# Dilated attention scores as 64-row matmuls instead of zero-padded 128-row ones, with two output banks in an expert layer

## The chip, the cores and the metric

The kernel runs on one core of a Trainium2 chip. The metric is the device time of one execution in microseconds (us). The kernel before takes 339.29 us, the median of three runs (339.09 to 340.91). The profile comes from one execution each time, so it has a span of its own (337.9 us for the kernel before, from the first to the last instruction).

A word used throughout: a **visit** is a stretch of consecutive matmuls that read only 64 (or fewer) of the 128 partitions, with matmuls over more than 64 partitions before and after it.

## The reference, cut to what matters

Eight batches of eight heads, 576 positions, head dimension 64. Heads 0 to 3 attend to the last 32 positions (here called plain), heads 4 to 7 to every fourth of the last 128 (dilated). The result goes through an expert layer with a swish of its own beta for each unit.

```python
def _attn_ref(q, k, v):                       # each 8 x 8 x 576 x 64, values x 0.1
    scores = np.matmul(q, k.transpose(0, 1, 3, 2)) / np.sqrt(64)
    rel = pos[:, None] - pos[None, :]
    mask_plain = (rel >= 0) & (rel < 32)
    mask_dil = (rel >= 0) & (rel < 128) & (rel % 4 == 0)
    ...                                       # masked softmax over keys
    return np.matmul(attn, v)

def _moe_ref(x, w_in, w_out, beta):           # x: 4608 x 512, w_in: 512 x 2048
    h = x @ w_in
    g = h * (1.0 / (1.0 + np.exp(-beta * h)))
    return g @ w_out
```

## The kernel before

The program is a fixed order of small steps. An attention batch is a list of step names: K and Q bring keys and queries (batches 0 and 1 by transposes on TensorE), `S` makes scores, `V` multiplies by values, `X` transposes the result into `xT`; `k`, `q`, `d`, `v` are copies on other engines, and W is a warm-up matmul whose result nobody reads. Batch 0 runs alone in the prologue; the batches after it are woven between the matmuls of the expert layer, whose nine stages of 512 tokens each begin with `h_ps` blocks (TensorE), a tanh (ScalarE) and a product g (VectorE), and end with `o_ps` blocks. The numbers in a step name are the pair of heads (2 and 3 are the dilated pairs) and the part of it.

```python
STEPS = (
    "S20 S21 S22 k0 S23 k1 V20 S30 q0 V21 S31 q1 V22 S32 q2 V23 S33 q3 V30 X20 S00 V31 S01 X21 V32 "
    "S02 V33 S10 V00 X30 S11 V01 S12 X31 V10 X00 V11 X01 X10 X11"
).split()
...
    psum_h = psum("psum_h", 2)
    psum_o = psum("psum_o", 1)      # one bank for output blocks
    psum_at = psum("psum_at", 5)    # five rotating banks for all of attention
```

Two dilated heads lie on the two halves of the partitions, 64 rows each. A score matmul uses all 128 rows: its keys are both heads' rows, and its queries are in `qzd`, where the other head's half is zero. One matmul of 192 columns then yields both heads. The price is the zeros, and the copies that spread the queries:

```python
    def spread_dil(b, hf, eng):
        rows = slice(64 * hf, 64 * hf + 64)
        copy_on(eng)(out=qzd[b % 2][rows, hf], in_=raw[b, "d"][rows])

    def step_q(b, x):
        tv = [transposes_p("q", y) for y in (x, x + 1)] if x < 2 else transposes_d("q", x)
        h = slice(2 * (x - 2), 2 * (x - 2) + 2)
        for n, hf in ((0, 0), (1, 1), (0, 1), (1, 0)):
            rows = slice(64 * hf, 64 * hf + 64)
            out = (q1[b][rows, x + n, hf].rearrange("p (a e) -> p a e", e=9) if x < 2 else
                   qzd[b][rows, hf, n, h].rearrange("p h (a w) -> p h a w", w=3))
            copy_on(nc.scalar if hf else nc.vector)(out=out, in_=tv[n][rows])

    def step_s(b, x, j):
        sc = bank().rearrange("p (a n) -> p a n", a=2)
        if x < 2:
            n, K, c = QT, P, 4 * QT * j
            mask = mask_p["PP" if j else "FP"][:].rearrange("p a b e u -> p a (b e u)")
        else:
            hf, rp = divmod(j, 2)
            n, K, c = DQ[hf], DK[hf], 4 * (hf * 2 * DQ[0] + rp * DQ[hf])
            mask = mask_d[hf][:].rearrange("p a b n -> p a (b n)")
        if b < 2:
            rhs = neg_d[hf][0:K].unsqueeze(1).to_broadcast([K, 4, n]) if x > 1 else (
                neg_p[:, 1:2].to_broadcast([K, 4, n]) if j else
                neg_p[:].unsqueeze(2).to_broadcast([K, 2, 2, n]))
            nc.tensor.matmul(sc[0:K, :, 0:2 * n], lhsT=ident_b[0:K, 0:K], rhs=rhs,
                             start=True, stop=False)
        for a in range(2):
            if x < 2:
                i = 2 * j + a
                if b < 2:
                    nc.tensor.matmul(
                        sc[:, a, 0:2 * n], lhsT=k1[b][:, x, i * QT:i * QT + P],
                        rhs=q1[b][:, x, :, i * QT:(i + 1) * QT], start=False, stop=a == 1)
                    continue
                for h2 in range(2):
                    h4 = 2 * x + h2
                    nc.tensor.matmul(
                        sc[:, a, h2 * n:(h2 + 1) * n],
                        lhsT=kz[b % 2][:, h4, i].rearrange("p e u -> p (e u)"),
                        rhs=qq[b % 2][:, h4, i].rearrange("p e u -> p (e u)"),
                        start=True, stop=True)
            else:
                h4 = 2 * (x - 2) + a
                nc.tensor.matmul(
                    sc[0:K, a, 0:2 * n],
                    lhsT=kd[b][:, rp, h4, DO[hf]:DO[hf] + K],
                    rhs=qzd[b % 2][:, :, rp, h4, hf * DQ[0]:hf * DQ[0] + n],
                    start=b > 1, stop=b > 1 or a == 1)
        w = pt[x][0:K, c:c + 4 * n].rearrange("p (a n) -> p a n", a=2)
        nc.scalar.activation(out=w, in_=sc[0:K, :, 0:2 * n], func=ACT.Exp, scale=SCALE)
        if b > 1:
            nc.gpsimd.tensor_tensor(out=w, in0=w, in1=mask[0:K], op=ALU.mult)
```

The two matmul groups of the expert layer, with the output block that goes into the single `o_ps` bank and is evicted by ScalarE:

```python
    def slot_h(t, fb, kts=None):
        if (t, fb) not in h_t:
            h_t[t, fb] = (bank() if (t == 0 or t == 1 and fb < 7) and fb % 3 else
                          psum_h.tile([P, NTOK], FP32, name="h_ps")[:])
        hps = h_t[t, fb]
        for kt in kts or (2, 3, 0, 1):
            nc.tensor.matmul(
                hps, lhsT=w_in_bf[:, kt, fb * P:(fb + 1) * P],
                rhs=xT[:, kt, t * NTOK:(t + 1) * NTOK],
                start=(kt == 2), stop=(kt == 1))
        if kts == (2, 3):
            return
        tnh = tnh_pool.tile([P, NTOK], BF16, name="tnh")
        nc.scalar.activation(
            out=tnh[:], in_=hps, func=ACT.Tanh, scale=beta_half[:, fb:fb + 1])
        g = g_pool.tile([P, NTOK], BF16, name="g")
        nc.vector.scalar_tensor_tensor(
            out=g[:], in0=tnh[:], scalar=1.0, in1=hps, op0=ALU.add, op1=ALU.mult)
        g_t[t, fb] = g

    ...

    def slot_o(t, tb, part):
        if part == 0:
            if t == NTT - 1 and tb % 2 or t == 0 and tb < 2:
                o_t[t, tb] = psum_h.tile([P, HD], FP32, name="h_ps")
            else:
                o_t[t, tb] = psum_o.tile([P, HD], FP32, name="o_ps")
        ops = o_t[t, tb]
        for fb in range(4 * part, 4 * part + 4):
            nc.tensor.matmul(
                ops[:], lhsT=g_t[t, fb][:, tb * P:(tb + 1) * P], rhs=w_out_bf[:, fb, :],
                start=(fb == 0), stop=(fb == NFB - 1))
        if part == 3:
            osb = osb_pool.tile([P, HD], FP32, name="osb")
            nc.scalar.mul(out=osb[:], in_=ops[:], mul=0.5)
            later.append([2, lambda: store(t * NTOK + tb * P, osb)])
```

The softmax here doesn't subtract the row's maximum and nothing guards it: scores larger than these inputs give would overflow.

## Time and profile before

| | kernel before |
|---|---|
| time, median of 3 | 339.29 us |
| span of the profiled run | 337.9 us |
| TensorE (PE) busy | 317.3 us, 94% |
| VectorE (DVE), ScalarE (ACT), GpSimd (POOL) busy | 58%, 59%, 39% |
| a settled batch (from about 132 us on) | 33.6 us |

The main views are shown in the prediction below, and each is explained there. Two further readings are needed for the result. The first is the clock row of the page: the span in 40 equal slices of some 8.4 us, each digit the granted TensorE clock in tenths of full speed.

```profile
PEclk9969999999999999999999999999999999999999
```

The 6 says that the third slice ran partly at half clock; the trace's clock records give 16.6 to 23.4 us. The second is the timeline of ScalarE at the first tanh, which ends the prologue: everything that delays it delays the whole kernel.

```profile
28.18 0.69 ACT L504 ACTIVATE tnh<-h_ps,beta_half 128x512 bf16<-128x512 f32 x1 [0.47 <-PE h_ps L497]
```

The columns of a timeline row are the start in us, the time to its end in us, engine, source line, operation, output and inputs, shapes, the number of instructions in the row, and in brackets how long the engine was idle before it and what ended that. The first tanh of each stage is a good milestone: its time in two traces, subtracted, shows in which stage time was lost.

### The profile page before, as it was taken

How to read it: one execution, taken by the hardware profiler on the slowest of the kernel's cores; microseconds unless marked ns; L12 is line 12 of the kernel's file. 1: busy time of each engine (PE TensorE's matmuls, PEld its weight loads, DVE VectorE, ACT ScalarE, POOL GpSimd, SP SyncE). 2: the span in 40 equal slices, each digit the busy share in tenths (PEclk: the TensorE clock that was granted, in tenths of full speed). 3: DMA queues.
4: the chain of work that ended last, by engine and by line, in shares of the span. 5: the costliest groups of instructions: out<-in, count | busy, mean ns of one | idle time of the engine just before them, and what ended most of it. 6: DMA issues, size and time to landing. Idle time of an engine off the chain costs nothing.

```text
span 337.9 us, 6328 instructions
## 1 busy us (share of the span) xinstructions
PE 317.3 (94%) x2406; PEld 167.5 (50%) x2406; DVE 195.3 (58%) x433; ACT 198.2 (59%) x380; POOL 131.4 (39%) x172
## 2 busy tenths in 40 slices
...
PEclk9969999999999999999999999999999999999999
...
GB/s 110 198 182 191 217 243 189 170 205 219 186 146 178 141 169 136 163 180 108 136 153 185 114 136 170 167 115 64 31 0 33 62 34 32 31 33 34 41 82 62
DMA packets 64783, 42.63 MB, mean 126 GB/s; under 512 B 48880, under 2 KB 58512, under 8 KB 64368
## 3 DMA queue, kind: packets, MB, share of 16 engines
...
q14 instruction: 12, 0.10, 0.1%
...
## 4 chain that ended last, share of the span: by engine, by line
PE 82%; DVE 7%; ACT 5%; DMA 2%; POOL 2%; issue 1%; POOLq 0%; ACTq 0%
PE o_ps L530 32%; PE h_ps L497 30%; PE h_ps L530 4%; PE at L436 3%; DVE g L507 3%; PE at L453 3%; PE at L497 3%; DMA xT<-in_k_dram 2%; PE at L403 2%; ACT osb L535 2%; PE at L410 2%; ACT tnh L504 2%; PE at L352 1%; DVE xs L443 1%; PE at L391 1%
## 5 line engine op out<-in xcount | busy, mean ns | idle before, releaser
L507 DVE SCALAR_TENSOR_TENSOR g<-tnh,h_ps 128x512 bf16<-128x512 bf16 x130 | 88.7, 684 | 90.3 <-ACT tnh L504 89.7
L497 PE MATMUL h_ps<-xT,w_in_bf 128*128 128x512 bf16 x520 | 130.9, 379 | 2.4 <-DVE g L507 2.1
L530 PE MATMUL o_ps<-w_out_bf,g 128*128 128x512 bf16 x512 | 128.9, 379 | 3.8 <-ACT osb L535 3.8
L504 ACT ACTIVATE tnh<-h_ps,beta_half 128x512 bf16<-128x512 f32 x130 | 89.3, 687 | 56.0 <-PE h_ps L497 51.9
L530 PEld LDWEIGHTS <-g 128*128 128x128 bf16 x576 | 52.3, 97 | 55.3 <-issue 6.1
L497 PEld LDWEIGHTS <-w_in_bf 128*128 128x128 bf16 x576 | 51.8, 98 | 51.4 <-issue 3.1
L416 ACT ACTIVATE pt<-at 128x384 bf16<-128x384 f32 (+2 forms) x112 | 47.7, 438 | 17.6 <-PE at L403 8.0
L418 POOL TENSOR_TENSOR pt<-pt,mask_d 96x384 bf16<-96x384 bf16 (+1 forms) x48 | 36.9, 778 | 48.4 <-ACT pt L416 47.7
L443 DVE TENSOR_TENSOR xs<-at,rcp 96x256 bf16<-96x256 f32 (+2 forms) x96 | 44.5, 464 | 10.9 <-PE at L453 6.9
L418 POOL TENSOR_TENSOR pt<-pt,mask_PP 128x384 bf16<-128x384 bf16 x24 | 22.8, 949 | 37.5 <-ACT pt L416 37.4
L535 ACT ACTIVATE osb<-o_ps 128x512 f32<-128x512 f32 x32 | 19.1, 597 | 24.1 <-PE o_ps L530 24.1
L436 PEld LDWEIGHTS <-pt 128*128 128x128 bf16 (+2 forms) x448 | 24.2, 98 | 14.3 <-DVE vd L323 1.2
L439 DVE RECIPROCAL rcp<-at 96x4 f32<-96x4 f32 (+2 forms) x96 | 16.9, 176 | 8.3 <-PE at L436 7.4
L453 PE MATMUL at<-ident_b,xs 96*128 96x96 bf16 (+1 forms) x224 | 18.2, 202 | 1.5 <-DVE xs L443 1.0
L410 PEld LDWEIGHTS <-kdT 128*96 128x96 bf16 (+1 forms) x128 | 14.3, 120 | 10.6 <-issue 1.2
L436 PE MATMUL at<-vd,pt 96*128 96x65 bf16 (+1 forms) x256 | 18.0, 195 | 1.1 <-DVE vd L323 1.0
L453 PEld LDWEIGHTS <-xs 96*128 96x128 bf16 (+1 forms) x224 | 13.4, 98 | 11.2 <-DVE xs L443 2.2
L410 PE MATMUL at<-qzd,kdT 128*96 128x192 bf16 (+1 forms) x128 | 17.9, 226 | 0.8 <-DVE qzd L276 0.8
L418 POOL TENSOR_TENSOR pt<-pt,mask_FP 128x384 bf16<-128x384 bf16 x12 | 10.9, 910 | 16.3 <-ACT pt L416 16.3
L530 PE MATMUL h_ps<-w_out_bf,g 128*128 128x512 bf16 x64 | 15.5, 379 | 1.1 <-DVE g L507 1.1
L463 ACT COPY xT<-at 128x288 bf16<-128x288 bf16 x24 | 9.0, 399 | 10.0 <-PE at L453 10.0
L403 PEld LDWEIGHTS <-kz 128*128 128x128 bf16 x144 | 9.9, 97 | 9.0 <-issue 2.0
...
## 6 DMA issues: line engine op xcount, KB each, us to landing
...
```

What stands on the lines that cost most here:

```text
L410: nc.tensor.matmul(sc[0:K, a, 0:2 * n], lhsT=kd[b][:, rp, h4, DO[hf]:DO[hf] + K], rhs=qzd[b % 2][:, :, rp, h4, hf * DQ[0]:hf * DQ[0] + n], ...
L416: nc.scalar.activation(out=w, in_=sc[0:K, :, 0:2 * n], func=ACT.Exp, scale=SCALE)
L418: nc.gpsimd.tensor_tensor(out=w, in0=w, in1=mask[0:K], op=ALU.mult)
L436: nc.tensor.matmul(pv[:, a, h2, :], lhsT=pt[x][0:K, c:c + P], rhs=rhs, start=True, stop=True)
L439: nc.vector.reciprocal(out=rcp[0:n, 0:m], in_=pv[0:n, :, :, D])
L443: nc.vector.tensor_tensor(out=xs_t[b, x, jx][:, a0:a0 + m], in0=pv[0:n, :, :, 0:D], in1=rcp[0:n, 0:m].unsqueeze(3).to_broadcast([n, m, 2, ...
L453: nc.tensor.transpose(xp[:, a * n:(a + 1) * n], xs[:, a].rearrange("p h d -> p (h d)"), ident_b[0:n, 0:n])
L497: nc.tensor.matmul(hps, lhsT=w_in_bf[:, kt, fb * P:(fb + 1) * P], rhs=xT[:, kt, t * NTOK:(t + 1) * NTOK], start=(kt == 2), stop=(kt == 1))
L504: nc.scalar.activation(out=tnh[:], in_=hps, func=ACT.Tanh, scale=beta_half[:, fb:fb + 1])
L507: nc.vector.scalar_tensor_tensor(out=g[:], in0=tnh[:], scalar=1.0, in1=hps, op0=ALU.add, op1=ALU.mult)
L530: nc.tensor.matmul(ops[:], lhsT=g_t[t, fb][:, tb * P:(tb + 1) * P], rhs=w_out_bf[:, fb, :], start=(fb == 0), stop=(fb == NFB - 1))
L535: nc.scalar.mul(out=osb[:], in_=ops[:], mul=0.5)
```

## The change

The intent is to make dilated scores without padded queries: each head's matmul reads only its own 64 partitions, so the zeroed query buffers, their copies and memsets go. One step now makes four matmuls of 96 (or 48) columns on one half of the partitions, instead of two of 192 (or 96) on all. The plain scores of batches 0 and 1, where the queries were padded as well, change in the same way. The attention now has four rotating banks instead of five, and output blocks have two instead of one, and the last output block is computed and stored by halves. The diff, cut to its core:

```diff
@@ -21,15 +21,15 @@
 ).split()
 
 FIRST = (
-    "W10 K2 W2 Q2 W3 K3 S20 S21 Q3 W2 S22 S23 z0 v0 S30 S31 S32 S33 V20 V21 K0 v1 V22 V23 V30 K1 X20 "
-    "V31 Q0 V32 V33 X21 S00 X30 S01 X31 S02 v4 S10 V00 S11 V01 S12 H0 v5 X00 V10 H1 X01 V11 X10 X11 z1 z2"
+    "W10 K2 W2 Q2 W2 K3 S20 S21 Q3 W2 S22 S23 v0 S30 S31 S32 S33 W2 V20 V21 K0 v1 V22 V23 V30 K1 X20 "
+    "V31 Q0 V32 V33 X21 S00 S01 X30 S02 S03 X31 v4 S10 S11 V00 S12 S13 V01 H0 v5 X00 V10 H1 X01 V11 X10 X11"
 ).split()
 SECOND = (
-    "K2 Q2 K3 Q3 v0 S20 v1 S21 S22 S23 K0 K1 S30 V20 S31 Q0 V21 S32 V22 S33 V23 V30 S00 "
-    "V31 X20 v2 S01 V32 S02 V33 S10 X21 S11 V00 X30 S12 V01 X31 V10 X00 V11 X01 X10 X11"
+    "K2 Q2 K3 Q3 v0 S20 S21 v1 S22 S23 K0 K1 S30 S31 V20 Q0 V21 S32 S33 V22 V23 V30 S00 S01 "
+    "V31 X20 v2 S02 S03 V32 V33 S10 S11 X21 V00 X30 S12 S13 V01 X31 V10 X00 V11 X01 X10 X11"
 ).split()
 THIRD = (
-    "d0 d1 v0 S20 S21 S22 k0 S23 v1 V20 S30 k1 V21 S31 q0 V22 S32 q1 V23 S33 q2 q3 V30 X20 S00 V31 "
+    "v0 S20 S21 S22 k0 S23 v1 V20 S30 k1 V21 S31 q0 V22 S32 q1 V23 S33 q2 q3 V30 X20 S00 V31 "
     "S01 X21 V32 S02 V33 v2 S10 V00 X30 S11 V01 S12 X31 V10 X00 V11 X01 X10 X11"
 ).split()
... (pools, buffers and memsets that only follow from this are cut)
-    psum_o = psum("psum_o", 1)
-    psum_at = psum("psum_at", 5)
+    psum_o = psum("psum_o", 2)
+    psum_at = psum("psum_at", 4)
...
@@ -270,10 +257,6 @@
 
     def copy_on(eng):
         return eng.copy if eng is nc.scalar else eng.tensor_copy
-
-    def spread_dil(b, hf, eng):
-        rows = slice(64 * hf, 64 * hf + 64)
-        copy_on(eng)(out=qzd[b % 2][rows, hf], in_=raw[b, "d"][rows])
 
     def spread_k(b, e, eng):
         half = raw[b, "k"][64 * e:64 * e + 64]
...
@@ -360,60 +344,53 @@
             copy_on(eng)(out=k1[b][:, x, WIN:].rearrange("p (a e) -> p a e", e=9),
                          in_=transposes_p("k", x))
         else:
-            h = slice(2 * (x - 2), 2 * (x - 2) + 2)
-            for rp, tv in enumerate(transposes_d("k", x)):
-                copy_on(nc.scalar if rp else nc.vector)(
-                    out=kd[b][:, rp, h].rearrange("p h (a w) -> p h a w", w=3), in_=tv)
-
+            evacuate_d("k", kd[b], x)
 
     def step_q(b, x):
-        tv = [transposes_p("q", y) for y in (x, x + 1)] if x < 2 else transposes_d("q", x)
+        if x > 1:
+            evacuate_d("q", qd[b], x)
+            return
+        for y in (x, x + 1):
+            copy_on(nc.scalar if y % 2 else nc.vector)(
+                out=q1[b][:, y].rearrange("p (a e) -> p a e", e=9), in_=transposes_p("q", y))
+
+    def evacuate_d(n, dst, x):
         h = slice(2 * (x - 2), 2 * (x - 2) + 2)
-        for n, hf in ((0, 0), (1, 1), (0, 1), (1, 0)):
-            rows = slice(64 * hf, 64 * hf + 64)
-            out = (q1[b][rows, x + n, hf].rearrange("p (a e) -> p a e", e=9) if x < 2 else
-                   qzd[b][rows, hf, n, h].rearrange("p h (a w) -> p h a w", w=3))
-            copy_on(nc.scalar if hf else nc.vector)(out=out, in_=tv[n][rows])
+        for rp, tv in enumerate(transposes_d(n, x)):
+            copy_on(nc.scalar if rp else nc.vector)(
+                out=dst[:, rp, h].rearrange("p h (a w) -> p h a w", w=3), in_=tv)
+
+
 
     def step_s(b, x, j):
-        sc = bank().rearrange("p (a n) -> p a n", a=2)
-        if x < 2:
-            n, K, c = QT, P, 4 * QT * j
-            mask = mask_p["PP" if j else "FP"][:].rearrange("p a b e u -> p a (b e u)")
+        t, r = divmod(j, 2)
+        rows = slice(64 * r, 64 * r + 64)
+        if x > 1:
+            n, m, K, c = DQ[t], 4, DK[t], 8 * DQ[0] * t + 4 * DQ[t] * r
+            ops = [(kd[b][rows, rp, 2 * (x - 2) + h2, DO[t]:DO[t] + K],
+                    qd[b][rows, rp, 2 * (x - 2) + h2, t * DQ[0]:t * DQ[0] + n])
+                   for rp in range(2) for h2 in range(2)]
+            mask = mask_d[t][:].rearrange("p a b n -> p (a b n)")
+            rhs = neg_d[t][0:K].unsqueeze(1).to_broadcast([K, 4, n])
+        elif b < 2:
+            n, m, K, c = QT, 3, P, (6 * t + 3 * r) * QT
+            ops = [(k1[b][rows, x, i * QT:i * QT + P], q1[b][rows, x, i * QT:(i + 1) * QT])
+                   for i in range(3 * t, 3 * t + 3)]
+            rhs = neg_p[:, 1:2].to_broadcast([K, 3, n]) if t else neg_p[:]
         else:
-            hf, rp = divmod(j, 2)
-            n, K, c = DQ[hf], DK[hf], 4 * (hf * 2 * DQ[0] + rp * DQ[hf])
-            mask = mask_d[hf][:].rearrange("p a b n -> p a (b n)")
+            n, m, K, c = QT, 4, P, 4 * QT * j
+            ops = [(kz[b % 2][:, 2 * x + h2, i].rearrange("p e u -> p (e u)"),
+                    qq[b % 2][:, 2 * x + h2, i].rearrange("p e u -> p (e u)"))
+                   for i in (2 * j, 2 * j + 1) for h2 in range(2)]
+            mask = mask_p["PP" if j else "FP"][:].rearrange("p a b e u -> p (a b e u)")
+        sc = bank()[0:K, 0:m * n]
         if b < 2:
-            rhs = neg_d[hf][0:K].unsqueeze(1).to_broadcast([K, 4, n]) if x > 1 else (
-                neg_p[:, 1:2].to_broadcast([K, 4, n]) if j else
-                neg_p[:].unsqueeze(2).to_broadcast([K, 2, 2, n]))
-            nc.tensor.matmul(sc[0:K, :, 0:2 * n], lhsT=ident_b[0:K, 0:K], rhs=rhs,
-                             start=True, stop=False)
-        for a in range(2):
-            if x < 2:
-                i = 2 * j + a
-                if b < 2:
-                    nc.tensor.matmul(
-                        sc[:, a, 0:2 * n], lhsT=k1[b][:, x, i * QT:i * QT + P],
-                        rhs=q1[b][:, x, :, i * QT:(i + 1) * QT], start=False, stop=a == 1)
-                    continue
-                for h2 in range(2):
-                    h4 = 2 * x + h2
-                    nc.tensor.matmul(
-                        sc[:, a, h2 * n:(h2 + 1) * n],
-                        lhsT=kz[b % 2][:, h4, i].rearrange("p e u -> p (e u)"),
-                        rhs=qq[b % 2][:, h4, i].rearrange("p e u -> p (e u)"),
-                        start=True, stop=True)
-            else:
-                h4 = 2 * (x - 2) + a
-                nc.tensor.matmul(
-                    sc[0:K, a, 0:2 * n],
-                    lhsT=kd[b][:, rp, h4, DO[hf]:DO[hf] + K],
-                    rhs=qzd[b % 2][:, :, rp, h4, hf * DQ[0]:hf * DQ[0] + n],
-                    start=b > 1, stop=b > 1 or a == 1)
-        w = pt[x][0:K, c:c + 4 * n].rearrange("p (a n) -> p a n", a=2)
-        nc.scalar.activation(out=w, in_=sc[0:K, :, 0:2 * n], func=ACT.Exp, scale=SCALE)
+            nc.tensor.matmul(sc, lhsT=ident_b[0:K, 0:K], rhs=rhs, start=True, stop=False)
+        for i, (lhsT, rhs) in enumerate(ops):
+            nc.tensor.matmul(sc[:, i * n:(i + 1) * n], lhsT=lhsT, rhs=rhs,
+                             start=b > 1, stop=b > 1 or i == m - 1)
+        w = pt[x][0:K, c:c + m * n]
+        nc.scalar.activation(out=w, in_=sc, func=ACT.Exp, scale=SCALE)
         if b > 1:
             nc.gpsimd.tensor_tensor(out=w, in0=w, in1=mask[0:K], op=ALU.mult)
 
... (step_v: only the columns of pt that it reads)
@@ -508,20 +485,25 @@
             out=g[:], in0=tnh[:], scalar=1.0, in1=hps, op0=ALU.add, op1=ALU.mult)
         g_t[t, fb] = g
 
-    def store(p0, osb):
+    def store(p0, osb, cols=slice(0, HD)):
 
         a = 0
         while a < P:
             b, p = divmod(p0 + a, S)
             r, s = divmod(p, CT)
             n = min(P - a, CT - s)
-            dst = out[b * S:(b + 1) * S].rearrange("(t T) d -> T t d", T=C)[r, s:s + n]
+            dst = out[b * S:(b + 1) * S].rearrange("(t T) d -> T t d", T=C)[r, s:s + n, cols]
             nc.sync.dma_start(out=dst, in_=osb[a:a + n])
             a += n
 
     def slot_o(t, tb, part):
+        if (t, tb) == (NTT - 1, 3):
+            last_o(t, tb, part)
+            return
         if part == 0:
-            if t == NTT - 1 and tb % 2 or t == 0 and tb < 2:
+            if t > NTT - 3 and tb:
+                o_t[t, tb] = psum_at.tile([P, HD], FP32, name="at")
+            elif t == 0 and tb < 2:
                 o_t[t, tb] = psum_h.tile([P, HD], FP32, name="h_ps")
             else:
                 o_t[t, tb] = psum_o.tile([P, HD], FP32, name="o_ps")
@@ -534,6 +516,26 @@
             osb = osb_pool.tile([P, HD], FP32, name="osb")
             nc.scalar.mul(out=osb[:], in_=ops[:], mul=0.5)
             later.append([2, lambda: store(t * NTOK + tb * P, osb)])
+
+
+    def last_o(t, tb, part):
+        hf, second = divmod(part, 2)
+        cols = slice(hf * HD // 2, (hf + 1) * HD // 2)
+        if not second:
+            o_t[t, tb] = psum_at.tile([P, HD], FP32, name="at")
+        ops = o_t[t, tb][:, 0:HD // 2]
+        for fb in range(8 * second, 8 * second + 8):
+            nc.tensor.matmul(
+                ops, lhsT=g_t[t, fb][:, tb * P:(tb + 1) * P], rhs=w_out_bf[:, fb, cols],
+                start=(fb == 0), stop=(fb == NFB - 1))
+        if second:
+            osb = osb_pool.tile([P, HD], FP32, name="osb")
+            if hf:
+                nc.vector.tensor_single_scalar(
+                    out=osb[:, 0:HD // 2], in_=ops, scalar=0.5, op=ALU.mult)
+            else:
+                nc.scalar.mul(out=osb[:, 0:HD // 2], in_=ops, mul=0.5)
+            store(t * NTOK + tb * P, osb[:, 0:HD // 2], cols)
 
     later = []
... (loads and places of the deferred steps)
```

## The prediction

> **What bounds the kernel now.** I read four views, from coarse to fine. First the page's head: the span of 337.9 us (timed 339.29) holds 317.3 us of matmuls.
>
> ```profile
> PE 317.3 (94%) x2406; PEld 167.5 (50%) x2406; DVE 195.3 (58%) x433; ACT 198.2 (59%) x380; POOL 131.4 (39%) x172
> ```
>
> TensorE is the only engine near full; VectorE and ScalarE have 40% to spare. An average can hide a stage with another limit, so the second view is the table by stage, one row for each batch of attention woven into the expert layer.
>
> ```profile
> 0.00:30.00 30.00, 24.57 (x280) 15.43 (x281) 18.29 (x63) 15.77 (x36) 21.50 (x41) 0.89 1.03 170
> 30.00:64.00 34.00, 32.71 (x341) 18.96 (x339) 23.78 (x51) 22.62 (x46) 17.99 (x26) 1.00 1.21 207
> 64.00:98.00 34.00, 29.26 (x232) 15.54 (x233) 23.94 (x51) 23.92 (x46) 15.20 (x19) 1.00 1.10 194
> ...
> 165.60:199.20 33.60, 33.21 (x253) 17.79 (x252) 21.47 (x48) 21.42 (x43) 16.10 (x18) 1.00 0.86 148
> ```
>
> The columns after the length are busy us of PE, weight loads, DVE, ACT and POOL. From 132 us on a batch takes 33.6 us and PE is busy for 33.21 of it: whatever is added to PE's stream there is added to the time. At 64 to 98 us PE is idle for 4.7 us, so something else limits there, and in the first 30 us too. The third view, the waits of PE, says which.
>
> ```profile
> PE o_ps L530 <- ACT osb L535: 3.8, 9, 0.7
> PE h_ps L497 <- DVE g L507: 2.1, 3, 1.1
> PE at L403 <- DVE qq L288: 1.6, 2, 1.3
> ```
>
> The first is the single output bank: the next output block starts only when ScalarE has evicted the one before (0.60 us each). The other two are VectorE's backlog at 64 to 116 us, where it copies keys and queries. Idle time understates a wait, because a matmul's modelled end lies well after its successor can start. So the fourth view is the timeline of PE, read from start to start.
>
> ```profile
> 194.04 0.34 PE L436 MATMUL at<-vp,pt 128*128 128x65 bf16 x6
> 194.76 1.02 PE L530 MATMUL o_ps<-w_out_bf,g 128*128 128x512 bf16 x4 [0.37 <-ACT osb L535]
> ...
> 165.84 0.33 PE L410 MATMUL at<-qzd,kdT 128*96 128x192 bf16 x2
> 166.00 1.03 PE L497 MATMUL h_ps<-xT,w_in_bf 128*128 128x512 bf16 x4
> ...
> 224.28 1.03 PE L530 MATMUL o_ps<-w_out_bf,g 128*128 128x512 bf16 x4
> 225.15 0.33 PE L403 MATMUL at<-qq,kz 128*128 128x96 bf16 x4
> 225.41 0.27 PE L453 MATMUL at<-ident_b,xs 48*128 48x48 bf16 x4
> 225.61 1.04 PE L497 MATMUL h_ps<-xT,w_in_bf 128*128 128x512 bf16 x4
> ```
>
> Six 65-column matmuls need some 0.18 us (29 ns each), but the next starts 0.72 us later: 0.54 us lost to the bank, not 0.37. Two 192-column score matmuls go in 0.16 us, four 512-column ones in 0.87: 82 and 216 ns, one column per 0.42 ns, weights hidden. Then the pair that decides this case: four 96-column matmuls should take 0.17 us, but the 48-row transposes start after 0.26; those should take 0.10 us at 25 ns, and the next 128-row matmul starts after 0.20. **Going into a matmul of at most 64 rows costs about 0.09 us, and coming back 0.10.** The same 0.10 stands before and after the other 48- and 64-row groups of this trace.
>
> **What the Trainium skill says.** "TensorEngine Tiling (Array Packing)", section Key Properties: "Mode switching requires drain". Tiles of 64 rows are another mode than 128, and the trace agrees with about 0.19 us per visit. Its section Gotcha 1: PSUM Pressure says that different row tiles must not use one PSUM bank at the same time; so the change gives each half of the partitions its own step and bank. "TensorE: Matmul & The Clock Gate", section Part 3: Packing small matmuls, says that matmuls start and end in program order; two halves overlap only if they are neighbours in the order. Its section on LDWEIGHTS makes the load's time that of its columns, not rows, so 64 rows load no faster. The trace has weight loads of 80 and 96 columns at 117 and 123 ns against 98 for 128, busy time that overlaps.
>
> **The change, part by part.**
> 1. *Scores.* A dilated step was two matmuls of 192 (or 96) columns over 128 rows, half of them zeros. It becomes four of 96 (or 48) over 64 rows. The columns stay: 2x192 = 4x96. Nothing is saved in streaming, as a step touches only one half. But a step is now a visit to the 64-row mode. I counted visits in the built program's order of PE instructions: 31 before, 105 after, 74 more: 46 in batches 2 to 7, where nearly every step stands alone between expert matmuls (two neighbours in all), 17 in batch 1, 11 in batch 0. The mask matmuls of batches 0 and 1 stay at 80 to 128 rows, so each step there switches too. At 0.19 us, plus 0.02 (my estimate) since the first weights inside a mode can't be loaded ahead: 74 x 0.21 = +15.5 us. The 48-column matmuls cannot go below the 25 ns seen, and their 80-column weights come no faster than some 38 ns, an estimate scaled from the 32 ns between 64-column transposes: 4 x 38 less 2 x 42 = 0.05 to 0.07 us for each of 32 steps, +2 us. Plain steps of batches 0 and 1 keep 9216 columns in all.
> 2. *Copies gone.* Twelve query copies on VectorE (0.56 us each, 6.8 in all) vanish, and half-height copies of batches 0 and 1 become full-height ones, half as many. VectorE isn't the bound after 116 us, so this pays only at 64 to 98 us (a start held 0.9 us by such a copy, three by backlog, 4 us in all) and in the prologue.
> 3. *Two output banks.* Nine waits, start to start 0.36 to 0.85 us: five of 0.54, two of 0.85, one of 0.36, one of 0.56, in all -5.3 us. The last two stages use the attention's banks, free by then, so these go too.
> 4. *Four rotating banks for five.* Value blocks are held about 2.1 us (first matmul to VectorE's end, at most 2.9); four allocations take about 3 us. It should just do: 0 to +1 us.
> 5. *Last block by halves.* The last matmul starts at 332.9 us, the eviction (0.60) at 333.4, then the store runs to 337.85. A half-width eviction and store end perhaps 0.5 us earlier: -0.5.
>
> What part of the +17.5 us is on the path? Batches 2 and 3 have 4 + 1.4 us of VectorE stalls: with PE slower and VectorE relieved most go, -4. In batch 0, ruled by loads until 14.7 us, I let most of 2.3 us hide and give the copies 1 us: -3. Small query waits of 0.18 us in later batches: -0.5. Sum: 17.5 + 0.5 - 5.3 - 4 - 3 - 0.5 - 0.5 = **+4.7 us, 344.0 us**. A settled batch should go from 33.6 to 8 x 0.21 + 0.25 - 0.54 - 0.1 = +1.3, about 34.9 us.
>
> **Rivals.**
> *The switches are hidden or don't come.* If 64-row steps cost no drain, -5.3, the copies and the tail leave about 331 us. For: the author meant a gain. Against: every 48- and 64-row group in the trace pays. Even if halves overlapped fully, they would have to be neighbours, which they aren't.
> *Switches cost in full everywhere, and four banks add a wait.* If batch 0 and the VectorE stalls absorb nothing: 339.3 + 17.5 - 5.8 + 1 = 352 us. Against: 4.7 us of idle PE at 64 to 98 us.
> *The clock in the prologue.* The page's clock row falls to 6 tenths in the third slice, 17 to 25 us, after PE idled. The new order puts warm-up matmuls just before the first value blocks, in a gap of 1 us. If that keeps the clock, 1 to 2 us are won; if more is lost, as much.
>
> **Range and chances.** Between these I put 338.5 to 349.5 us for 8 in 10. 2% slower is 346.1, 2.1 us above my value, with an uncertainty of about 4: 0.32. 2% faster is 332.5, only with the first rival: 0.05.
>
> **What would show it.** Steps 1: in the timeline, from a dilated step's first matmul to the next 128-row start about 0.26 us, and 0.09 lost ahead of it; a settled batch near 34.9 us. Step 3: no wait of output blocks on ScalarE. Step 2: at 64 to 98 us PE idle under 2 us. Step 4: no wait of scores on VectorE or ScalarE's evictions. The prediction is wrong if a 64-row step follows a 128-row matmul without the 0.09 us, or if the first 64 us shift by over 4 us.

## The result and the profile after

The changed kernel is slower: 350.3 us, the median of four runs (349.66 to 351.87), against 339.19 us for four runs of the kernel before in the same rounds. The ratio is 1.033 (95% interval 1.027 to 1.039). The prediction was 344.0 us with a range to 349.5, most likely within 2%: wrong in size, right in its sign.

The page's head and clock row of the changed kernel:

```profile
PE 334.0 (96%) x2535; PEld 173.1 (50%) x2579; DVE 183.6 (53%) x408; ACT 197.1 (57%) x378; POOL 128.7 (37%) x172
PEclk9758999999999999999999999999999999999999
```

TensorE has 17 us more of busy time, VectorE 12 us less. The clock row has a longer dip: 7, 5, 8 where it was 9, 6, 9; by the records, half clock lasts from 12.5 to 29.6 us, 17.1 us instead of 6.8. The timed runs say the same: by their mean clocks, the changed kernel spends 14.6 to 21.7 us at half clock, the kernel before 6.7 to 12.9 us in 30 of the 35 runs beside the experiments. (The records know only full and half clock, so the time at half clock is 2 x (1 - mean clock) x span, which includes a piece of about 1 us after the last matmul and leaves out the 4 to 7 us before the first record, where the warm-up matmuls start 0.43 us apart, twice the 0.216 us of full clock.) (The trace has 2535 matmuls for 2579 weight loads. The missing ones are records that were lost, not work: they look like holes of 0.22 us that end on "issue".)

The table by stage, in the same windows as before (length, then busy us of PE, weight loads, DVE, ACT and POOL, then clock, DMA share and GB/s):

```profile
0.00:30.00 30.00, 28.08 (x291) 17.17 (x294) 11.86 (x49) 12.96 (x30) 21.71 (x41) 0.72 1.03 175
30.00:64.00 34.00, 32.48 (x317) 17.48 (x322) 19.35 (x40) 20.84 (x40) 18.22 (x28) 1.00 1.15 205
64.00:98.00 34.00, 29.86 (x239) 15.13 (x242) 22.16 (x49) 23.85 (x47) 9.39 (x13) 1.00 0.93 163
165.60:199.20 33.60, 33.23 (x249) 17.04 (x253) 19.70 (x45) 20.25 (x40) 15.48 (x18) 1.00 0.75 135
```

In the first 30 us PE is busy 3.5 us longer and the mean clock is 0.72 instead of 0.89. At 64 to 98 us PE is still idle for 4.1 us, where the prediction expected under 2. That window holds earlier work than before, as the changed kernel is 6.3 us behind by then; over stages 2 and 3, from first tanh to first tanh, PE's idle time goes from 6.0 us to about 4.9 (lost records count as idle). These are the longest single waits of PE that are left in them, with the total, the number and the longest:

```profile
PE at L390 <- DVE qq L271: 1.3, 1, 1.3
...
PE at L413 <- ACT vp L303: 0.9, 1, 0.9
PE at L390 <- ACT xT L444: 0.8, 1, 0.8
```

Each is one wait, for a copy of queries (at 89.9 us), a cast of values (98.0) and an eviction (121.3). The first is one that the prediction had shown (1.6 us in two waits before) and expected to go. The waits on g fell from 2.1 us to 0.9, and the 0.8 us on a `qzd` copy went. No output block waits for ScalarE any more; the row with 3.8 us is gone. What each score step costs is seen in PE's timeline of a settled batch:

```profile
175.12 0.81 PE L474 MATMUL h_ps<-xT,w_in_bf 128*128 128x512 bf16 x3 [0.16 <-issue]
175.86 0.38 PE L390 MATMUL at<-qdT,kdT 64*96 64x96 bf16 x4
176.17 1.04 PE L512 MATMUL o_ps<-w_out_bf,g 128*128 128x512 bf16 x4
```

Three 512-column matmuls take 0.65 us from start to start (216 ns each), so the next could start at 175.77; the 64-row step starts at 175.86, 0.09 later. Its four matmuls of 96 columns should take 0.17 us, but the next matmul over 128 rows starts after 0.31, 0.14 late. That is 0.23 us for this visit. And the milestone that ends the prologue:

```profile
32.00 0.69 ACT L481 ACTIVATE tnh<-h_ps,beta_half 128x512 bf16<-128x512 f32 x1 [0.47 <-PE h_ps L474]
```

It comes 3.82 us later than before. The same milestone of every stage gives the account below. "Stage 1" is the distance from the first tanh of expert stage 0 to that of stage 1, and so on; each entry is this distance minus that of the kernel before, in us, in the profiled run. The rows below the first are the experiments of the next section.

| run | prologue | stage 1 | stage 2 | stage 3 | each of stages 4 to 7 | rest, three steps | sum |
|---|---|---|---|---|---|---|---|
| changed kernel | +3.82 | +2.50 | +0.45 | +0.45 | +1.43 | -2.38 | +10.56 |
| all_padded | +1.35 | +0.02 | -0.48 | -0.50 | -0.53 | -2.38 | -4.13 |
| b0_padded | +1.83 | +2.50 | +0.45 | +0.45 | +1.43 | -2.29 | +8.68 |
| wide0 | +1.07 | +2.50 | +0.45 | +0.45 | +1.43 | -2.39 | +7.80 |
| wide0v | +3.03 | +2.50 | +0.45 | +0.45 | +1.43 | -2.39 | +9.78 |
| pairs | +4.18 | +2.50 | +2.06 | +0.28 | +0.14 | -2.39 | +7.21 |
| early | +3.94 | +3.46 | -0.92 | -0.45 | +1.43 | -2.39 | +9.38 |
| best | +0.60 | +0.65 | -1.28 | -1.23 | -0.36 | -2.40 | -5.10 |

The stages 4 to 7 agree within 0.01 us in all traces of one order of steps. The prologue does not: it depends on where the clock falls in that one run. Its scatter is 1 to 3 us, so for the prologue I also use the timed runs.

### The profile page after: what moved, and what is told of

The parts are those of the page before. It is cut to its first block, busy times and chain, and to the rows that moved or that the text cites. A ratio compares the mean times of both kernels' runs of the same rounds, so it can differ in the third digit from the quotient of the medians.

```text
span 348.4 us, 6617 instructions
## 1 busy us (share of the span) xinstructions
PE 334.0 (96%) x2535; PEld 173.1 (50%) x2579; DVE 183.6 (53%) x408; ACT 197.1 (57%) x378; POOL 128.7 (37%) x172
## 4 chain that ended last, share of the span: by engine, by line
PE 88%; DVE 4%; ACT 3%; issue 2%; DMA 1%; POOL 1%; DVEq 0%; ACTq 0%; POOLq 0%
PE h_ps L474 32%; PE o_ps L512 27%; PE at L390 8%; PE at L512 5%; PE at L413 4%; PE at L430 3%; PE at L474 3%; PE h_ps L512 2%; PE at L388 2%; ACT tnh L481 1%; DVE g L484 1%; DMA xT<-in_k_dram 1%; PE at L336 1%; PE at L528 1%; DVE xs L420 1%
## 5 line engine op out<-in xcount | busy, mean ns | idle before, releaser
L474 PE MATMUL h_ps<-xT,w_in_bf 128*128 128x512 bf16 x491 | 127.9, 380 | 3.4 <-issue 1.0
L512 PE MATMUL o_ps<-w_out_bf,g 128*128 128x512 bf16 x437 | 111.5, 379 | 0.6 <-issue 0.2
L512 PEld LDWEIGHTS <-g 128*128 128x128 bf16 x560 | 49.1, 97 | 48.3
L393 ACT ACTIVATE pt<-at 128x384 bf16<-128x384 f32 (+3 forms) x116 | 49.4, 431 | 27.1 <-PE at L390 26.3
L517 ACT ACTIVATE osb<-o_ps 128x512 f32<-128x512 f32 x28 | 16.7, 597 | 18.6 <-PE o_ps L512 15.5
L390 PEld LDWEIGHTS <-kdT 64*96 64x96 bf16 (+1 forms) x256 | 14.9, 118 | 20.9 <-issue 19.7
L390 PE MATMUL at<-qdT,kdT 64*96 64x96 bf16 (+1 forms) x256 | 22.0, 206 | 0.0
L512 PE MATMUL at<-w_out_bf,g 128*128 128x512 bf16 x79 | 19.2, 379 | 0.1
L444 ACT COPY xT<-at 128x384 bf16<-128x384 bf16 (+1 forms) x32 | 12.6, 395 | 5.0 <-PE at L430 5.0
L474 PE MATMUL at<-xT,w_in_bf 128*128 128x512 bf16 x56 | 14.4, 388 | 0.1
```

Of the source, the lines that this page charges most:

```text
L390: nc.tensor.matmul(sc[:, i * n:(i + 1) * n], lhsT=lhsT, rhs=rhs, start=b > 1, stop=b > 1 or i == m - 1)
L393: nc.scalar.activation(out=w, in_=sc, func=ACT.Exp, scale=SCALE)
L474: nc.tensor.matmul(hps, lhsT=w_in_bf[:, kt, fb * P:(fb + 1) * P], rhs=xT[:, kt, t * NTOK:(t + 1) * NTOK], start=(kt == 2), stop=(kt == 1))
L512: nc.tensor.matmul(ops[:], lhsT=g_t[t, fb][:, tb * P:(tb + 1) * P], rhs=w_out_bf[:, fb, :], start=(fb == 0), stop=(fb == NFB - 1))
```

## The experiments

Sixteen kernels ran, all with the correct result by the comparison. They are built from one source in which each part of the change can be switched, and which gives the instruction orders of both kernels exactly. Line numbers in their traces therefore differ. The diffs are given in short.

### all_padded: the change without its 64-row scores

```diff
-dilated and plain scores on 64 rows                # as in the changed kernel
+step_q, step_s, spread_dil, qzd and the step orders of the kernel before
 psum_o 2 banks, psum_at 4 banks, last block by halves   # kept
```

> Everything of the change but the scores: all batches keep the zero-padded 128-row scores, with two output banks, four rotating banks and the last block by halves. Theory 1 (the whole loss comes from the 64-row scores; banks and halves gain): 339.2 - 5.3 (nine bank waits) - 0.8 (end of the last block, as the two traces show it) = 333 us, a settled batch 33.62 - 0.54 = 33.1 us. Rival (four rotating banks for five are too few, and part of the loss is theirs): 336 us or more, with waits of PE on evictions of the rotating banks that the kernel before has not.

Measured: 335.52 us (334.84 to 336.92), ratio 0.987 (0.983 to 0.992). So the other parts of the change are a gain, 1.3%. It is smaller than the expected one (333 us): in the profile the prologue is 1.35 us longer than before, with 10.2 us at half clock instead of 6.8. And the 64-row scores cost the difference to 350.3: 14.8 us by the medians. A settled batch takes 33.09 us, 0.53 less than before, which is the output-bank wait of the prediction (0.54). The list of PE's waits has no wait of scores on the evictions of others, so from stage 1 on four banks for five cost nothing here.

### b0_padded: 64-row scores everywhere but in batch 0

```diff
-batch 0: scores on 64 rows, changed order FIRST
+batch 0: zero-padded queries, FIRST of the kernel before
```

> The changed kernel with batch 0 alone on zero-padded 128-row scores and the order of steps of before. Theory 1 (the 3.8 us that the prologue loses come from TensorE running at half clock for 17 us instead of 7, and the 64-row scores of batch 0 are why the clock is not granted): clock at half for about 7 us, the first tanh back from 32.0 to about 28.2 us, 350.3 - 3.8 = 346.5 us. Rival (the clock is lost for another reason, such as full-height copies or fewer banks): half clock for 17 us again and 349.5 to 350.5 us.

Measured: 347.9 us (347.41 to 348.23), ratio 1.023 (1.020 to 1.027). From stage 1 on it is identical to the changed kernel (table above). Batch 0 is worth about 2 us in the profile and 2.4 by the medians. That lies between the two expectations (346.5, and 349.5 or more); half clock is back at 10.2 us. So the prologue term of the prediction is a wrong one. This run changes the order of steps in batch 0 too; wide0, below, does not.

### visits64 and visits128: one extra small matmul per dilated step

Both are the kernel before, zero-padded scores and all, with one matmul of 16 columns after each dilated step of batches 2 to 7. It reads 64 rows in one and 128 in the other, and its result is not used. The difference of the two is the price of a visit by itself.

```diff
+            nc.tensor.matmul(sc[0:K, 1, 2*n:2*n+16],
+                lhsT=kd[b][0:64, 0, 2*(x-2)+1, DO[hf]:DO[hf]+K],    # 0:128 in visits128
+                rhs=kd[b][0:64, 0, 0, 0:16], start=True, stop=True)
```

> The kernel before with one added matmul of 64 rows and 16 columns at the end of each dilated step of batches 2 to 7 (48 in all, into columns of the bank that nothing reads). Theory 1 (each visit to 64-row matmuls costs some 0.2 us of PE's stream): a settled batch 33.62 + 8 x 0.2 = 35.2 us, in all 339.2 + 48 x 0.2 less what the VectorE stalls of batches 2 and 3 absorb (0 to 2 us) = 347 to 349 us. Rival (a visit is free, and the settled batches lose by doubled weight loads): 340.5 us as its control.

> Control of the run before it: the same 48 added matmuls of 16 columns, but over 128 rows. Both theories: 25 to 30 ns each, 339.2 + 1.3 = 340.5 us, a settled batch 33.85 us.

Measured: visits64 348.15 us (346.84 to 350.62), ratio 1.025 (1.018 to 1.032); visits128 341.32 us (339.61 to 342.02), ratio 1.003 (0.999 to 1.008). PE's timeline of visits64:

```profile
204.22 0.33 PE L451 MATMUL at<-qzd,kdT 128*96 128x192 bf16 x2
204.48 0.21 PE L457 MATMUL at<-kdT 64*96 64x16 bf16 x1
204.62 1.04 PE L580 MATMUL h_ps<-xT,w_in_bf 128*128 128x512 bf16 x4
```

And of visits128:

```profile
201.59 0.33 PE L451 MATMUL at<-qzd,kdT 128*96 128x192 bf16 x2
201.75 0.17 PE L457 MATMUL at<-kdT 128*96 128x16 bf16 x1
201.78 1.02 PE L580 MATMUL h_ps<-xT,w_in_bf 128*128 128x512 bf16 x4
```

From the scores to the next expert matmul it is 0.40 us with a visit and 0.19 without. The settled stage is longer by 1.79 us and 0.175 us, so eight visits (the dilated steps of a batch) cost 1.62 us, **0.202 us each**. The prediction had 0.19, read from transposes alone, and 0.21 with its allowance. This step held. What makes the 0.2 us no run separates: at both edges of a visit the weight load, too, starts only 1 to 4 ns before its matmul, where between 128-row matmuls it starts some 0.2 us ahead.

### warm and warm2: more warm-up matmuls in the changed prologue

```diff
-"W10 K2 W2 Q2 W2 K3 S20 S21 Q3 W2 S22 S23 v0 S30 S31 S32 S33 W2 V20 V21 K0 ..."
+"W10 K2 W2 Q2 W2 K3 S20 W1 S21 W1 Q3 W2 S22 W1 S23 W1 v0 S30 W1 S31 W1 S32 W1 S33 W2 V20 V21 W4 K0 ..."   # warm
+"W10 K2 W2 Q2 W2 K3 S20 S21 Q3 W4 S22 W1 S23 v0 S30 W1 S31 S32 S33 V20 V21 W4 K0 ..."                     # warm2
```

> The changed kernel with eleven more idle 128-row, 512-column matmuls in batch 0: one after each dilated step but the last, four before the first plain keys. Nothing else changes. Theory 1 (the prologue's loss is the granted clock, which too little array work has cost): half clock for 7 to 10 us instead of 17, the first tanh at 28.5 to 30 us instead of 32.0, in all 347 to 348 us of 350.3. Rival (the visits themselves cost the prologue its time): the clock may return, but the first tanh comes no earlier, 350 to 352 us.

> The changed kernel with the idle 128-row matmuls of batch 0 moved and six more of them, fewer than the run warm's eleven, and most of them where PE waits for loads anyway (before the first value blocks and before the first plain keys). Theory 1 (the half clock costs the prologue about 2 us, and in the run warm the added matmuls cost as much): clock held to 19 us or more and first tanh at 30 to 31 us instead of 32.0, in all 348.5 to 349.5 us. Rival (the clock costs nothing here, since the chain through evictions sets the prologue): first tanh at 32 us, 350.3 us.

Measured: warm 350.06 us (349.81 to 350.36), ratio 1.032 (1.027 to 1.037); warm2 350.02 us (348.98 to 350.85), ratio 1.030 (1.024 to 1.034). Both are misses as cures. The clock did come back: the mean granted clock of warm's timed runs leaves 7 to 8 us at half clock. But the first tanh of warm is 3.89 us late, as in the changed kernel: eleven more matmuls at 0.216 us are 2.4 us of PE. At the first step after them warm is 2.05 us behind the changed kernel, and by the first tanh the faster clock has just made that up. In warm2, with six more, the first tanh comes at 31.09 us, 0.91 earlier, but its times show no gain clear of noise. Clock bought with extra matmuls cost here about what it brought.

### pairs, alternate and fours: neighbouring steps

In pairs the two halves of a dilated step stand next to each other in program order; in alternate their eight matmuls take turns, one half and then the other, in two banks; in fours all four steps of a pair of heads stand in a row. Only batches 2 to 7 are changed.

```diff
-"S20 S21 S22 k0 S23 k1 V20 S30 q0 V21 S31 q1 V22 S32 q2 V23 S33 q3 V30 ..."
+"P20 k0 P21 k1 V20 P30 q0 V21 q1 V22 P31 q2 V23 q3 V30 ..."     # pairs, alternate: P = two halves
+"F2 k0 k1 V20 q0 V21 F3 q1 V22 q2 V23 q3 V30 ..."               # fours: F = four steps
```

> The changed kernel with the two halves of each dilated step of batches 2 to 7 back to back: 24 visits to 64-row matmuls in place of 46, the same matmuls otherwise, issued half by half. Theory 1 (0.20 us per visit, as the added-visit run and its control show): a settled batch 35.06 - 4 x 0.20 = 34.26 us, in all 350.3 - 22 x 0.20 = 345.9 us. Rival (the loss lies in the eight matmuls and their weight loads, not in the visit): settled batch 34.9 to 35.1 us, 350 us.

> As the run with pairs, but the eight matmuls of a pair are issued in turn, one of the lower half of the partitions, one of the upper, to two banks. If matmuls of different halves overlap when they are neighbours: a pair of 96 columns takes some 0.18 instead of 0.35 us, one of 48 columns 0.15 instead of 0.30, a settled batch 0.65 us below that of pairs, 33.6 us, in all some 342 us. If they don't: as pairs, 345.9 us.

> The changed kernel with all four dilated score steps of a head pair back to back in batches 2 to 7: 2 visits to 64-row matmuls per batch instead of 4 in the run with pairs (and 8 in the change). From the trace of pairs, a visit with one pair takes 0.41 us (96 columns) or 0.37 us (48), in which the halves overlap; one visit with both should take 0.57 us: a settled batch 33.77 - 2 x 0.21 = 33.35 us, in all some 344 us. Rival (a group of four takes all four rotating banks at once and waits for evictions): a settled batch 33.8 us or more, with waits of dilated scores on evictions.

Measured: pairs 347.15 us (346.69 to 347.78), ratio 1.024 (1.017 to 1.030); alternate 345.92 us (344.84 to 346.84), ratio 1.020 (1.014 to 1.025); fours 351.8 us (350.4 to 353.49), ratio 1.035 (1.030 to 1.041). PE's timeline of pairs:

```profile
176.30 1.03 PE L655 MATMUL o_ps<-w_out_bf,g 128*128 128x512 bf16 x4
177.25 0.34 PE L503 MATMUL at<-qdT,kdT 64*80 64x48 bf16 x8
177.53 1.04 PE L615 MATMUL h_ps<-xT,w_in_bf 128*128 128x512 bf16 x4
```

Eight matmuls of a pair need 0.28 us to the next expert matmul, where four alone needed 0.26 in the changed kernel: the second half is nearly free. In the records the two halves' matmuls start 13 ns apart and take turns, although kernel.py issues four of one half and then four of the other: the first two records both carry the wait for a bank, the last two both the signal of the end. A settled batch falls from 35.06 to 33.77 us (alternate: 33.73), with 24 visits left in batches 2 to 7 instead of 46. That is the rival of the prediction ("even if halves overlapped fully, they would have to be neighbours"), now made true, and it still loses: all_padded's batch takes 33.09. Pairs gained less in time than 4 x 1.3 us because stage 2 took 1.6 us more: in both runs the clock fell to half for 3.4 us near 90 us, after a wait of 2.05 us for a query copy.

In fours the settled batch is back at 35.08 us. The scores were moved ahead of the query copies that they need, and PE waits for them:

```profile
PE at L524 <- DVE qq L346: 8.0, 6, 2.0
PE at L524 <- ACT pt L527: 2.2, 6, 0.6
```

The second row is new too: four steps in a row outrun the evictions.

### qpool and early: why VectorE's relief did not help in batches 2 and 3

Part 2 of the prediction expected the stalls at 64 to 116 us to go. PE's timeline and VectorE's timeline of the changed kernel show the largest that stayed:

```profile
88.29 0.34 PE L430 MATMUL at<-ident_b,xs 96*128 96x96 bf16 x4
89.93 0.34 PE L390 MATMUL at<-qq,kz 128*128 128x96 bf16 x4 [1.30 <-DVE qq L271]
```

```profile
88.23 0.69 DVE L484 SCALAR_TENSOR_TENSOR g<-tnh,h_ps 128x512 bf16<-128x512 bf16 x1 [0.51 <-ACT tnh L481]
88.94 0.92 DVE L271 COPY qq<-qpT 64x1152 bf16<-64x1152 bf16 x2
```

VectorE has no backlog here: it was idle for 0.51 us. The query copies stand behind a g in VectorE's order, the g waits for a tanh, and the tanh for PE. It is a wait on order. Taking work off VectorE does not move it, and a slower PE moves it along. Two runs try this: qpool puts the query copies of batches 2 and 3 on GpSimd; early moves the copies forward in the order of steps.

```diff
-    nc.vector for q0 to q3 of batches 2 and 3
+    nc.gpsimd                                                       # qpool
-"S20 S21 S22 k0 S23 k1 V20 S30 q0 V21 S31 q1 V22 S32 q2 V23 S33 q3 V30 ..."
+"S20 S21 k0 S22 k1 S23 V20 q0 S30 V21 q1 S31 V22 q2 S32 V23 q3 S33 V30 ..."   # early, THIRD likewise
```

> The changed kernel with the eight query copies of batches 2 and 3 on GpSimd in place of VectorE. The prediction let 4 us of PE's stalls at 64 to 132 us vanish; the traces show 0.9 us of loss there instead of 2.3 of gain. Theory (the remaining stalls, 1.5 us in batch 2 and 1.0 in batch 3 of plain scores on the last query copy, come from the order on VectorE: the copy stands behind the expert layer's multiply, which waits for a tanh and that for PE): the wait of scores on VectorE's copy is gone, the two batches together 1.5 to 2.5 us shorter, 348 to 349 us. Rival (another link, such as ScalarE's casts, holds the same place): 350 to 351 us.

> The changed kernel with the key and query copies of batches 2 to 7 two or three steps earlier in the order of steps, so that the last query copy comes before the last dilated score step; the copies stay on VectorE. Theory (in batches 2 and 3 PE waits for the first plain scores because the last copy stands behind a multiply that waits for a tanh and for PE, an order and not a lack of VectorE time): the waits of 1.3 us in batch 2 and 0.8 us in batch 3 go, the two batches end 1.5 to 2 us earlier, 348.5 us. Rival (VectorE's work itself is too much there): the wait turns up at the expert layer's h_ps or at value blocks, 350 to 351 us.

Measured: qpool 351.2 us (349.85 to 351.8), ratio 1.035 (1.029 to 1.040). It tells little: a copy takes 1.14 us on GpSimd against 0.46 on VectorE, and PE now waits 2.7 us for it, so one wait took the place of another. Early: 348.8 us (348.01 to 349.52), ratio 1.026 (1.021 to 1.031). Its stages 2 and 3 are 1.37 and 0.90 us shorter than those of the changed kernel, and the wait is gone from PE's timeline at the same place:

```profile
89.49 0.34 PE L594 MATMUL at<-ident_b,xs 96*128 96x96 bf16 x4
89.66 0.34 PE L524 MATMUL at<-qq,kz 128*128 128x96 bf16 x4
```

The copies are the same in number and size, on the same engine; they even took longer (0.72 us on average, against 0.53). Only their place changed, and PE's idle time in stages 2 and 3 fell from about 4.9 us to 2.2. So it was the order. (Stage 1 of early is 0.96 us longer: in that run the half clock lasted until 33.9 us.)

### rows64: the kernel before, warm-up matmuls over half the rows

Why is the clock lost for longer? The rivals are the idle rows of 64-row matmuls and the pauses around visits. This run keeps all of the kernel before and changes only the rows that the warm-up matmuls read.

```diff
-nc.tensor.matmul(warm_ps[:], lhsT=warm_w[:, 0:P], rhs=warm_w[:], start=True, stop=True)
+nc.tensor.matmul(warm_ps[:], lhsT=warm_w[0:64, 0:P], rhs=warm_w[0:64, :], start=True, stop=True)
```

> The kernel before with one edit: its warm-up matmuls, which the prologue issues while it waits for data, read 64 partitions instead of 128; same number, same 512 columns, same places, result unused. Theory (the granted clock follows how many rows of the array work, not only how long it is busy): the first grant of full clock at 5 to 6.5 us comes late or not at all, a half-clock stretch of well over the 7 to 10 us of the kernel before shows in the prologue, and the span is 1 to 5 us longer. Rival (the clock follows only whether the PE streams, and the half-clock stretch of the changed kernel comes from the pauses at its visits): grant and half-clock stretch as before, 339 us within 1 us.

Measured: 341.27 us (341.01 to 342.81), ratio 1.006 (0.999 to 1.013). Ten warm-up matmuls take 4.45 us in both kernels. In the kernel before the first record of full clock comes at 6.35 us; here, at 25.64 us. PE's timeline of rows64, at the first scores:

```profile
1.27 4.45 PE L616 MATMUL o_ps<-warm_w 64*128 64x512 bf16 x10 [1.27 <-DVE neg_d L204]
...
9.56 0.53 PE L482 MATMUL at<-qzd,kdT 128*96 128x192 bf16 x2
9.88 0.53 PE L463 MATMUL at<-neg_d,ident_b 96*96 96x384 bf16 x1
```

And the same steps in the kernel before:

```profile
8.57 0.33 PE L410 MATMUL at<-qzd,kdT 128*96 128x192 bf16 x2
8.74 0.33 PE L391 MATMUL at<-neg_d,ident_b 96*96 96x384 bf16 x1
```

Two matmuls of 192 columns take 0.32 us to the next start, against 0.17: half clock. (The page's clock row of rows64 reads 9 throughout, because it has no record before 25.64 us; the durations tell the truth.) In all 17 other traces, whose first warm-up matmuls read 128 rows, the first record of full clock comes at 4.25 to 7.24 us. A stream that never pauses, over 64 rows, did not earn the clock that the same stream over 128 rows earns. The theory holds in that a stream's rows count. Its cost was small: 12.5 us more at half clock delay the first tanh by 1.65 us, since loads rule much of the prologue.

### wide0 and wide0v: the rows of batch 0's scores, without and with pauses

rows64 does not show that rows are what loses the clock in the changed kernel itself. In wide0 the score matmuls of batch 0 read all 128 rows, the same number and columns as in the changed kernel; heads are mixed, so the result is wrong. (The comparison passed it nevertheless, presumably because with inputs of 0.1 the scores are so near zero.) wide0v adds one 16-column matmul over 64 rows after each of these steps, so each step is a visit again.

```diff
-        rows = slice(64 * r, 64 * r + 64)
+        rows = slice(0, P) if b == 0 else slice(64 * r, 64 * r + 64)
+        if b == 0:                                                  # wide0v only
+            nc.tensor.matmul(raw_bank[0:K, m*n:m*n+16], lhsT=ops[0][0][0:64],
+                             rhs=ops[0][1][0:64, 0:16], start=True, stop=True)
```

> The changed kernel with the score matmuls of batch 0 over all 128 partitions instead of 64: same number, columns, order, banks, no visits in batch 0's scores; the result of batch 0 is wrong on purpose, as heads are mixed. Theory (the half-clock stretch comes from the idle rows): stretch back to about 10 us, mean loss of clock as in b0_padded, about 347.5 us. Rival 1 (it comes from the pauses at the visits): also back, about 347.5; the run beside this one separates them. Rival 2 (it has another cause, such as the order of loads or the copies): 350 us, 14 to 20 us at half clock.

> As wide0, with one 16-column matmul over 64 partitions after each score step of batch 0, so that every step is a visit again, with all its pauses, while the score columns keep all rows busy. Theory (idle rows): half-clock stretch about 10 us as in wide0, the time up only by the visits themselves, 16 x 0.2 us of which part hides: 347.5 to 349. Rival (pauses): 14 to 20 us at half clock in most runs, 350 us or more.

Measured: wide0 347.39 us (345.57 to 347.81), ratio 1.019 (1.013 to 1.025); wide0v 349.35 us (349.11 to 349.96), ratio 1.026 (1.019 to 1.033). At half clock, worked out from the mean clock of each timed run as above:

| kernel | us at half clock, four runs each |
|---|---|
| changed kernel | 14.6, 17.4, 18.1, 21.7 |
| wide0v | 10.4, 11.8, 11.8, 14.6 |
| wide0 | 6.9, 6.9, 10.4, 10.4 |
| kernel before, seven runs beside these | 10.2 to 12.8, one 19.8 |

Other runs with the changed prologue agree with the first row (early 17.3 to 20.2 us, qpool and fours 13.9 to 21.7). Making all rows work takes about 6 us off the stretch although all pauses are there (wide0v), and taking the pauses away as well some 3 us more. Both rivals have a share; the idle rows have the larger one. The time lies a little above what the theory expected of wide0v (347.5 to 349). The table by stage gives both a mean clock of 0.83 in the first 30 us, against 0.72 in the changed kernel; this is the row of wide0v:

```profile
0.00:30.00 30.00, 27.37 (x312) 17.97 (x313) 12.47 (x51) 13.37 (x31) 21.75 (x41) 0.83 1.02 173
```

With the same time at half clock, 10.2 us by the records (though 2.8 us later in wide0v), the profiles of these two differ by the visits: the first tanh comes at 29.25 and 31.21 us. By the order of matmuls in the two traces there are 24 visits before the first tanh in wide0v and 10 in wide0. **Fourteen visits delay the first tanh by 1.96 us, of the 2.8 that 14 x 0.202 makes.** The timed runs agree (345.57 to 347.81 us against 349.11 to 349.96), but there wide0v is also at half clock for some 3 us longer.

The timelines tell which of the visits hide. This is PE's timeline of wide0, at the first plain keys of batch 0 and at its first expert matmul:

```profile
14.73 0.98 PE L412 MATMUL at<-ident_b,xT 64*64 64x64 bf16 x18 [2.14 <-DMA xT<-in_k_dram]
...
25.31 0.59 PE L640 MATMUL h_ps<-xT,w_in_bf 128*128 128x512 bf16 x2
```

And of wide0v:

```profile
14.45 0.65 PE L412 MATMUL at<-ident_b,xT 64*64 64x64 bf16 x18
...
26.85 1.02 PE L644 MATMUL h_ps<-xT,w_in_bf 128*128 128x512 bf16 x2
```

| start in us | kernel before | wide0 | wide0v | changed kernel |
|---|---|---|---|---|
| plain keys of batch 0 | 14.73 | 14.73 | 14.45 | 14.45 |
| plain scores of batch 0 | 20.20 | 20.49 | 19.95 | 20.21 |
| first expert matmul | 24.45 | 25.31 | 26.85 | 27.25 |
| first tanh | 28.18 | 29.25 | 31.21 | 32.00 |

Seven of the fourteen visits belong to dilated steps, before the plain keys. They are hidden: wide0 and the kernel before wait there for a load (2.14 and 1.31 us), the other two do not, and at the plain scores they are not behind. The seven visits of the plain steps come after that. From the plain scores to the first expert matmul it is 4.82 us in wide0 and 6.90 in wide0v, 2.08 us more, where 7 x 0.202 makes 1.41: they are paid in full. (The matmuls that wide0v adds, and 0.4 us that wide0 has at full clock, are in the 2.08 too.)

From wide0v to the changed kernel there are 0.79 us in the profiles, 1.0 by the medians and 2.4 by the ratios (0.7% of 340): that is what remains for the clock. The intervals of the two ratios overlap, so its size is not clear of noise. (Mean times less the 6.7 us of the later stages put the prologue at +4.5 us for the changed kernel, +2.1 for wide0v and -0.3 for wide0, each within about 2 us.)

### best and best2: what comes out of it

best is all_padded with the order of early, and with warm-up matmuls at 128 rows in a gap of the prologue; best2 has the early order in batches 2 and 3 only.

```diff
-"... S30 S31 S32 S33 V20 V21 K0 ..."
+"... S30 S31 S32 S33 W4 V20 V21 W5 K0 ..."
-"S20 S21 S22 k0 S23 k1 V20 S30 q0 ..."
+"S20 S21 k0 S22 k1 S23 V20 q0 S30 ..."     # all batches from 2 on; in best2 only 2 and 3
```

> All batches on zero-padded 128-row scores, two output banks, four rotating, the last block by halves (the run all_padded, 335.5 us), with the copies of batches 2 to 7 earlier as in the run early, and nine idle matmuls where PE waits for loads in batch 0. All theories: at most 335.5 us. If order and clock matter as I think, the waits on query copies (2 us) and 1 us of the prologue go: 333 us.

> Run best with its order of early query copies only in batches 2 and 3 and the order of the kernel before in batches 4 to 7. Theory (the early order costs 0.17 us a settled batch against all_padded, 33.26 to 33.09, and is worth its 1.3 and 1.2 us only in batches 2 and 3): settled distance 33.09, four batches x 0.17 = 0.7 us less than best, about 332.8 us. Rival (the 0.17 is the scatter of two builds): as best, 333.5 us.

Measured: best 333.51 us (333.11 to 334.45), ratio 0.982 (0.978 to 0.986); best2 333.36 us (333.04 to 335.86), ratio 0.983 (0.976 to 0.989). Both beat both kernels, by 1.8% against the kernel before. In the profile best2 has the settled batch of all_padded, 33.09 us against 33.26, as its theory said; by the medians the two cannot be told apart, and the expected 332.8 us was not reached. The profiled run of best2 is its slowest, with 10.2 us at half clock and a first tanh at 31.50 us; best, with the same prologue, had 6.8 us and 28.78. That is the scatter of the prologue in one picture.

## Why the prediction was right or wrong

The table below sets the account of the result against the prediction's terms. The prediction summed by parts; I split its sum by stage. Of its 74 visits the traces have 14 before the first tanh, 14 in stage 1, and 7 or 8 in each stage from 2 to 7 (46). At 0.21 us, with 0.25 us a batch for its small columns and less its own waits and copies, that gives the second column: for the prologue 2.9 + 0.25 - 3, for stages 2 and 3 together 15 x 0.21 + 0.5 - 1.1 - 4 - 0.2.

| term | predicted | measured | by which run |
|---|---|---|---|
| prologue (batch 0) | about +0.2 | +3.8 | profile; b0_padded, wide0, wide0v |
| stage 1 (batch 1) | about +3.2 | +2.5 | profile |
| stages 2 and 3 | about -1.6 | +0.9 | profile; early |
| stages 4 to 7, each | +1.3 | +1.43 | profile; visits64 against visits128 |
| last three steps (output banks and halves) | about -2.6 | -2.4 | profile |
| four banks for five | +0.5 | about 0 | all_padded |
| output bank, a settled batch | -0.54 | -0.53 | all_padded |

**Steps that held.** A visit costs 0.202 us (predicted 0.19 to 0.21). The settled batch went to 35.06 us (predicted 34.9). The wait of output blocks on ScalarE went, and all_padded shows its worth to 0.01 us. Weights of 64 rows load no faster (118 ns on average, 120 before), as it said. The sign followed from this. Of the rivals, "switches cost in full everywhere" (352 us) came nearest, though its wait of four banks did not show. The rival "switches are hidden" fell, and pairs showed that its condition, neighbours, is real but not enough.

**The step that failed most: batch 0.** The prediction wrote "In batch 0, ruled by loads until 14.7 us, I let most of 2.3 us hide and give the copies 1 us: -3". It was mis-sized by about 3.6 us. (It also split its visits wrongly, 11 for batch 0 and 17 for batch 1; the traces have 14 and 14.) The loads explain half of the batch only. Up to the plain scores the changed kernel is level with the one before (20.21 against 20.20 us): the seven visits of the dilated steps did hide in the wait for loads. But the plain steps come after 20 us, where no load is awaited, and there nothing hid: to the first expert matmul it is 7.04 us instead of 4.25, and from there to the first tanh 4.75 instead of 3.73. wide0v against wide0 puts 1.96 us of this down to visits. The rest I put down mostly to the clock, which is at half until 29.6 us instead of 23.4. The prediction had it as a rival worth "1 to 2 us" either way, for warm-up matmuls and idle gaps; what it did not have is that a 64-row stream counts for less. rows64 shows that mechanism by itself, and the half-clock times of wide0v that it is at work here; its cost, 0.8 us (profile) to 2.4 us (times), is not clear of noise. How these two split exactly stays open, because one run's prologue moves by 1 to 3 us with the clock's windows. The prediction's own sign of being wrong, a shift of the first 64 us by over 4 us, did show: the first tanh of stage 1 comes 6.3 us later.

**The second: batches 2 and 3.** "With PE slower and VectorE relieved most go, -4" was wrong in its mechanism. Of the 4 us PE's idle time in these stages fell by about 1.1, mostly the waits on g and `qzd`. What stayed were waits on order, not on backlog, and there a relieved VectorE waits for the tanh. early shows it: same work, other place, 2.3 us back in two stages. The wait of 0.83 us in batch 3 that the profile puts down to an eviction of `xT` is of the same kind: the query copy had ended only 0.05 us before the eviction, and in early, with the same four banks, the wait is gone.

**In the other direction:** stage 1 cost 0.7 us less than its visits and columns make. I did not find what absorbs a part of them, and no run separates it.

Together: +3.6 in the prologue, -0.7 in stage 1, +2.5 in stages 2 and 3, +0.5 in the four settled ones, +0.2 in the last steps and -0.5 for the banks make 5.6 us. The prediction's +4.7 and these are +10.3, against +10.56 in the profile and +11.1 by the medians.

## What to carry to other kernels

Halving a matmul's rows saved nothing on TensorE here (96-column matmuls start 45 ns apart over 64 rows and 43 over 128) unless the other half worked at the same moment: count how often the order goes into the 64-row mode and back, and multiply by some 0.2 us, before counting the copies it saves. A wait for loads hides such costs only up to where the last load is awaited, so look at which steps come after it. Then ask of each wait whether it is a backlog (less work helps) or an order (only another place helps); the idle time of the awaited engine just before tells. And where a prologue loses the full clock, padding with zeros can be worth its rows (10.4 to 11.1 us at half clock in b0_padded, 14.6 to 21.7 in the changed kernel): look at the clock row, and at the duration of one known matmul where the row has no record.

## What the Trainium skill lacked or had wrong

- "TensorEngine Tiling (Array Packing)", Key Properties, says that a change of mode drains TensorE, but not for how long. The runs show 0.202 us for a visit to 64 rows between 128-row matmuls (visits64 against visits128), and 0.09 us before and 0.14 after a step of four 96-column matmuls in the changed kernel.
- "TensorE: Matmul & The Clock Gate", Part 3, says matmuls start and end in strict program order. In pairs the matmuls of two halves take turns, 13 ns apart, although kernel.py issues four of one half before the four of the other. The halves overlap without being alternated by hand (pairs 33.77 us a batch, alternate 33.73).
- The same page, Part 1, has the clock follow how busy the PE has been, in windows of 3.4 us; this case's half-clock stretches are multiples of 3.41 us (6.83, 10.24, 17.07), which agrees. It does not say that the rows in use count. In rows64 the first record of full clock comes at 25.64 us instead of 6.35 with half the rows in the warm-up matmuls, and with all rows in batch 0's scores (wide0v) the time at half clock is 10.4 to 14.6 us, where the changed kernel has 14.6 to 21.7.
- The same page, Part 1, warns that clock events in a trace are not to be trusted without a second check. No page says that a clock row can read full because records are missing: rows64 reads 9 in the first 25 us, and its 192-column score matmuls take twice as long as those of the kernel before.
